# Where the first reads of g and of rounded w_out, and one raw slice of w_out, stand in SP's queue of a retention and SiLU kernel

## The chip, the cores and the metric

The kernel runs on one core of a Trainium2 chip. The metric is the device time of one execution in microseconds, given as the median of several runs. A core has five engines that run side by side, each through its own queue in order: TensorE (PE) multiplies matrices, VectorE (DVE) and ScalarE (ACT) work element by element, GpSimd (POOL) copies here, and SyncE (SP) issues nearly all DMA transfers.

## The reference

Two blocks in a row. A recurrent retention: for each of 4 batches and 8 heads a 64 x 64 state decays and takes in one outer product per step, over 768 steps.

```
for t in range(S):
    state = gamma[None, :, None, None] * state + einsum('bhd,bhe->bhde', k[:, :, t], v[:, :, t])
    y[:, :, t] = scale * einsum('bhd,bhde->bhe', q[:, :, t], state)
x = y.transpose(0, 2, 1, 3).reshape(3072, 512)
h = x @ w_in                       # 512 x 2048
g = h * (1.0 / (1.0 + exp(-h)))    # SiLU
return g @ w_out                   # 2048 x 512
```

q, k and v are float32. The two weight matrices come in as 64-bit floats and are rounded on the chip.

## The kernel before, in words

**Units and groups.** The sequence is cut into 6 chunks of 128 steps. A unit is one chunk of one batch (24 units); its attention is computed in a "visit", whose three phases belong to three units that follow each other. The 4 units of a chunk c give one block xt[c] of 512 rows of x. Group c is what this block costs in the first product: 16 products (c, f), one for each slice f of 128 columns of w_in. The first two groups and half of group 2 are interleaved with the first units; the list `steps` holds the order of the products. From (3,0) on the groups run one after the other, with one visit after every fourth product of groups 3 and 4. Group 5 has no visits.

**Numbers as sums.** A product of float32 quality is made of three products of rounded planes: each operand is split into a high, a low and a mixed plane. `product_in(c, f)` issues eight matmuls into a PSUM bank ha and four into hb (L666). `close_steps` then takes them out: ScalarE copies ha into one of three buffers hs (L676, pool `hpool`), VectorE subtracts hb (L681), ScalarE applies SiLU (L686). The banks ha and hb of successive products go round three banks, so ha of product n+2 takes the bank of hb of product n, and hb of product n+1 the bank of ha of product n.

**g goes through memory.** `put_g(1)` (L689, store at L692) stores all finished tiles of g but the newest and keeps the store's instruction in `stored[0]`. A buffer hs is free again once its store has landed. In the output stage `get(n)` (L698, read at L705) reads the tiles back in order, and `split(n)` (L722) makes three planes of each: ScalarE L731, VectorE L733 and L734. `G_AHEAD` = 4 reads run ahead of the splits, and 3 splits ahead of the products (L1007).

**w_out goes through memory as well.** The 32 slices of both weights (16 of w_in, 16 of w_out) are taken one at a time by `take_w` at the products in the list `takes`. `convert_w` (L226) rounds a slice of 64-bit words in one ScalarE and six VectorE instructions (L202; L205, L208, L212, L215, L218, L223), and asks for the raw slice two further on: at once through `load_w` (L172; a slice of w_out is one transfer of 512 KB, L188), or, when `patient[0]` is set, by putting it into the list `waiting`, which the main loop empties later. A rounded slice of w_out is stored (`store_w`, L288). In group 5 `get_w(f)` (L708, read at L713) reads rounded slices back, `W_READ` = 4 ahead, and `w_out(f)` (L716) splits slice f into planes: ScalarE L120, VectorE L123, ScalarE L126, VectorE L128, and asks for slice f + 4. The low plane goes through one single buffer (tag wl of the pool `conv`).

**Late x.** The block of group 2 is made of values that were stored and are read back by `late_y` (L598) and split by `late_x` (ScalarE L569, VectorE L572 and L575).

**Transposes.** For units from 14 on, q and k are turned by DMA: GpSimd arranges words (`part_t`, L420), SP issues a transposing transfer for q and one for k (`turn_t`, L431), ScalarE joins the words (`join_t`, L438).

**What sets the order.** In the part that the change touches, TensorE's order is the program's. The other engines' queues are put in order by a scheduler when the program is built, which moves an instruction ahead when its inputs and buffers allow it by its own model of time. `with tc.issue_after(ins):` holds it back: what the block issues on the engine of `ins` stays behind `ins`. After the build every engine's queue is fixed.

The main loop (L943 to L985) issues for every product, in this order: the product, `put_g(1)`, `store_w()`, the slice to take, the visit, transposes and loads. In group 5 it adds the reads of w_out at f = 0, a split of w_out for f up to 11, the first four reads of g at f = 10, and the first three splits of g at f = 13 to 15.

Of the kernel before, what the change touches and what calls it, by code (L numbers as in the profile page):

```python
# [33 lines left out]
def kernel(  # L34
# [35 lines left out]
    NF = DF // 128  # L70
# [72 lines left out]
    LATER = 4 * B + 2  # L143
# [115 lines left out]
    taken, patient = [0], [False]  # L259

    def take_w(after=None, parts=False):

        i = taken[0]
        taken[0] += 1
        if i >= 2 * NF:
            return
        with queue(after) if after else ExitStack():
            rounded = convert_w(i)

        def finish():  # L270
            w32 = rounded()
            if i < NF:
                list(split_w(i, w32, "wi", scale, w_sb))
            else:
                to_store.append((i - NF, w32))

        if parts:
            behind_next.append(finish)
        else:
            with queue(after) if after else ExitStack():  # L280
                finish()
# [3 lines left out]
    def store_w():  # L285
        while to_store:
            f, w32 = to_store.pop(0)
            nc.sync.dma_start(out=wo_dram[f], in_=w32)  # L288
# [101 lines left out]
    def scale_k(n):  # L390
        if 0 <= n < len(units):
            t = kqv["k"][n]
            if units[n][0] == NC - 1:
                t = t[:D]
            if 2 * B + 1 < n < 3 * B + 2:

                def half(heads):
                    for h in heads:
                        nc.scalar.activation(out=t[:, h, :], in_=t[:, h, :], func=AF.Copy,
                                             scale=gk[:, units[n][0], h : h + 1])  # L400

                half(range(H // 2))
                behind_copy.append(lambda: half(range(H // 2, H)))
                return
            g = gk[: t.shape[0], units[n][0], :].unsqueeze(2).to_broadcast([t.shape[0], H, D])
            nc.vector.tensor_tensor(out=t, in0=t, in1=g, op=ALU.mult)
# [8 lines left out]
    def part_t(n, after=None):  # L415

        for name, (p, tag, bufs) in (("q", (ld, "kf", 3)), ("k", (one, "kt", 2))):
            src = kqv[name].pop(n) if name == "q" else kqv[name][n]
            t = p.tile([128, 2 * H * D], U16, tag=tag, name=f"{name}p_{n}", bufs=bufs)
            i = nc.gpsimd.tensor_copy(  # L420
                out=t.rearrange("p (w h d) -> p w h d", w=2, h=H),
                in_=src.bitcast(U16).rearrange("p h (d w) -> p w h d", w=2)).ins
            if after is not None:
                tc.add_manual_dep(i, after.name, mybir.DependencyInfo(
                    mybir.DependencyClass.Sync, mybir.DependencyReason.DATA), reason="later")
            planes[name, n] = t

    def turn_t(n):
        for name, (p, tag, bufs) in (("q", (ld, "qf", 2)), ("k", (one, "qt", 3))):
            t = p.tile([128, 2 * HP, C], U16, tag=tag, name=f"{name}w_{n}", bufs=bufs)  # L430
            turned_by[:] = [nc.sync.dma_start_transpose(out=t, in_=planes.pop((name, n))).ins]  # L431
            turned[name, n] = t

    def join_t(name, n):

        to, bufs = (qt, 3) if name == "q" else (kt, 2)
        to[n] = one.tile([128, HP, C], FP32, tag=f"{name}t", name=f"{name}t_{n}", bufs=bufs)
        nc.scalar.copy(out=to[n].bitcast(U16).rearrange("p a (t w) -> p w a t", w=2),  # L438
                       in_=turned.pop((name, n)).rearrange("p (w a) t -> p w a t", w=2))
# [217 lines left out]
    pending, stored = [], []  # L657

    def product_in(c, f):
        close_in(c, f, *multiply(c, f))  # L660
# [28 lines left out]
    def put_g(keep):  # L689
        while len(pending) > keep:  # L690
            c, f, g = pending.pop(0)
            stored[:] = [nc.sync.dma_start(out=g_dram[c, f], in_=g).ins]  # L692
# [5 lines left out]
    def get(n):  # L698
        if n >= len(order):
            return  # L700
        c, f = order[n]
        name = "kvqkvkqv"[n % 8]
        g = ld.tile([128, NT], FP32, tag=f"{name}f", name=f"gr_{c}_{f}",
                    bufs=2 if name == "q" else 3)
        nc.sync.dma_start(out=g, in_=g_dram[c, f])  # L705
        got[n] = g

    def get_w(f):  # L708
        if f < NF:
            tag = "kqkqq"[f % 5]  # L710
            t = one.tile([128, DM], FP32, tag=f"{tag}t", name=f"wr_{f}",
                         bufs=2 if tag == "k" else 3)
            nc.sync.dma_start(out=t, in_=wo_dram[f])  # L713
            w_got[f] = t
# [24 lines left out]
    G_AHEAD = 4  # L739
    W_READ = 4  # L740
# [163 lines left out]
    half = NF // 2  # L904
# [7 lines left out]
    steps = pairs + three + rest + last + groups  # L912
# [22 lines left out]
    turns_at = {first_far + 2: FAR}  # L935
# [7 lines left out]
    for n, (c, f) in enumerate(steps):  # L943
        if n in scales_at:
            behind_next.append(lambda m=scales_at[n]: scale_k(m))
        if n in joins_at:
            behind_copy.insert(0, lambda m=joins_at[n]: [join_t(name, m) for name in "qk"])
        if n in parts:
            behind_next.append(lambda m=parts[n]: part_t(m, taken_out[0]))
        patient[0] = steps.index((3, 0)) <= n < max(turns_at) + 2  # L950
        product_in(c, f)
        put_g(1)
        store_w()
        if (c, f) in takes:
            take_w(taken_out[0], n < len(pairs + three))
        behind.get((c, f), lambda: None)()
        if n in turns_at:
            turn_t(turns_at[n])
            if turns_at[n] >= LATER:
                with tc.issue_after(turned_by[0]):  # L960
                    load("k", turns_at[n] + 1), load("q", turns_at[n] + 1)
        if turns_at.get(n - 1, 0) >= LATER:
            with tc.issue_after(stored[0]):
                load("v", turns_at[n - 1] + 1)
        if turns_at.get(n - 2, 0) >= LATER:
            with tc.issue_after(stored[0]):
                while waiting:
                    load_w(waiting.pop(0))
        for name, m in loads_at.get(n, ()):
            load(name, m)  # L970
        if c == NC - 1:
            if f == 0:
                for i in range(W_READ):
                    get_w(i)
            if f < NF - 4:
                w_out(f)
            if f >= NF - 6:
                if f == NF - 6:
                    for n in range(G_AHEAD):
                        get(n)  # L980
                if f >= NF - S_AHEAD:
                    split(f - NF + S_AHEAD)
    put_g(0)

    for c in range(NC):  # L985
# [9 lines left out]
        for f in range(NF):  # L995
            n = c * NF + f
# [21 lines left out]
        for b in range(B):  # L1018
# [11 lines left out]
            n = 2 if b == B - 1 else 1  # L1030
# [36 lines left out]
```

## Time and profile before

| what | value |
|---|---|
| median of 3 runs | 621.18 us (618.72 to 621.54) |
| profiled execution | 620.76 us, its span 618.9 us |
| TensorE busy | 601.6 us, 97% of the span |
| VectorE, ScalarE, GpSimd busy | 424.6, 315.7, 29.1 us |
| share of TensorE in the chain that ended last | 73% |
| transfers on SP's queue | 102.79 MB in 141392 packets |
| stores of g (96 of 256 KB), median issue to landing | 3.4 us |
| reads of g (96 of 256 KB) | 2.7 us |
| reads of rounded w_out (16 of 256 KB) | 3.5 us |
| raw slices of w_out (16 of 512 KB) | 5.0 us |
| granted TensorE clock | 0.999 |

The span is the time from the first to the last instruction of the profiled execution; 1.9 us of its own time lie around it. Busy times are sums over the whole span and hide that stages differ. The chain that ended last is followed back from the last instruction, at each step to what released it; a DMA in it is a transfer that something waited for. In the tables by stretches the columns are each engine's busy time in the stretch with the number of its instructions, and then the granted clock, the DMA share and the rate. Products of group 5 begin at 309.24 us and 2.72 us apart; the output products begin at 352.85 us.

### The profile page before, as it was taken

How to read it: one execution, taken by the hardware profiler on the slowest of the kernel's cores; microseconds unless marked ns; L12 is line 12 of the kernel's file. 1: busy time of each engine (PE TensorE's matmuls, PEld its weight loads, DVE VectorE, ACT ScalarE, POOL GpSimd, SP SyncE). 2: the span in 40 equal slices, each digit the busy share in tenths (PEclk: the TensorE clock that was granted, in tenths of full speed). 3: DMA queues.
4: the chain of work that ended last, by engine and by line, in shares of the span. 5: the costliest groups of instructions: out<-in, count | busy, mean ns of one | idle time of the engine just before them, and what ended most of it. 6: DMA issues, size and time to landing. Idle time of an engine off the chain costs nothing.

```text
span 618.9 us, 13462 instructions
## 1 busy us (share of the span) xinstructions
PE 601.6 (97%) x5360; PEld 494.6 (80%) x5360; DVE 424.6 (69%) x731; ACT 315.7 (51%) x595; POOL 29.1 (5%) x85
## 2 busy tenths in 40 slices
PE   6898999999999999999999999999999999999997
PEld 5777787888778888887788888888888888888886
DVE  4998889889977777785699783645635453654631
ACT  6677896676667567665588642312221221412311
POOL 3000000100031111120000000000000000000000
PEclk9999999999999999999999999999999999999999
DMA  9998874784789699999777552533524433442301
GB/s 193 221 227 208 220 216 158 202 241 169 250 217 222 184 265 241 275 233 292 273 227 257 193 147 68 169 104 92 180 70 132 140 102 103 141 132 89 116 1 68
DMA packets 144334, 108.88 MB, mean 176 GB/s; under 512 B 101136, under 2 KB 109584, under 8 KB 144272
## 3 DMA queue, kind: packets, MB, share of 16 engines
q1 hardware_dynamic: 141392, 102.79, 59.7%
q10 hardware_dynamic: 2880, 5.24, 2.3%
q8 instruction: 42, 0.69, 0.5%
q14 instruction: 20, 0.16, 0.1%
HBM read 66.06 MB, written 36.70 MB: 166 GB/s over the span
## 4 chain that ended last, share of the span: by engine, by line
PE 73%; DVE 5%; DMA 2%; ACT 2%; issue 1%; SPq 1%; DVEq 0%; POOLq 0%; ACTq 0%
PE o L1007 21%; PE ha L666 18%; PE oa L1007 14%; PE hb L666 10%; PE ob L1007 7%; PE y L513 2%; DMA gd<-g 1%; DVE g L681 1%; DMA yr<-yd 1%; SPq L431 1%; PE sc L474 1%; PE sc L464 1%; DVE ca L218 1%; DVE xt L572 0%; ACT g L676 0%
## 5 line engine op out<-in xcount | busy, mean ns | idle before, releaser
L666 PE MATMUL ha<-xt,wi 128*128 128x512 f32 x768 | 193.7, 394 | 1.3 <-ACT xt L569 0.7
L666 PEld LDWEIGHTS ha<-xt,wi 128*128 128x128 f32 x768 | 141.8, 188 | 33.5 <-ACT xt L569 1.1
L1007 PE MATMUL o<-wo,gs 128*128 128x512 f32 x564 | 143.2, 389 | 0.0
L733 DVE TENSOR_TENSOR gs<-gr,gs 128x512 fp32r<-128x512 f32 x96 | 62.1, 685 | 90.3 <-ACT gs L731 90.3
L1007 PEld LDWEIGHTS o<-wo,gs 128*128 128x128 f32 x564 | 105.9, 188 | 21.9
L731 ACT ACTIVATE gs<-gr 128x512 fp32r<-128x512 f32 x96 | 53.6, 621 | 134.2 <-issue 131.9
L1007 PE MATMUL oa<-wo,gs 128*128 128x512 f32 x376 | 115.8, 389 | 0.0
L666 PE MATMUL hb<-xt,wi 128*128 128x512 f32 x384 | 103.2, 390 | 1.9 <-ACT g L676 0.9
L681 DVE TENSOR_TENSOR g<-g,hb 128x512 f32<-128x512 f32 x96 | 65.6, 683 | 37.1 <-ACT g L676 24.7
L666 PEld LDWEIGHTS hb<-xt,wi 128*128 128x128 f32 x384 | 71.8, 188 | 18.4 <-ACT g L676 1.8
L686 ACT ACTIVATE g<-g 128x512 f32<-128x512 f32 x96 | 60.1, 627 | 46.2 <-DVE g L681 46.2
L1007 PEld LDWEIGHTS oa<-wo,gs 128*128 128x128 f32 x376 | 70.6, 188 | 14.7
L1007 PE MATMUL ob<-wo,gs 128*128 128x512 f32 x188 | 73.7, 392 | 0.0
L676 ACT ACTIVATE g<-ha 128x512 f32<-128x512 f32 x96 | 56.7, 591 | 28.5 <-PE ha L666 11.9
L734 DVE SCALAR_TENSOR_TENSOR gs<-gs 128x512 fp32r<-128x512 f32 x96 | 62.0, 683 | 0.0
L1007 PEld LDWEIGHTS ob<-wo,gs 128*128 128x128 f32 x188 | 35.3, 188 | 8.7 <-DVE o L1025 1.6
L202 ACT ACTIVATE ca<-wf 128x512 f32<-128x512 f32 x32 | 21.4, 668 | 8.0 <-DVE cw L223 5.0
L218 DVE SCALAR_TENSOR_TENSOR ca<-wf,ca 128x512 f32<-128x512 uint32 x32 | 22.7, 710 | 0.5
L1024 ACT ACTIVATE o<-o 128x512 f32<-128x512 f32 x10 | 6.0, 598 | 33.4 <-PE o L1007 33.0
L482 DVE TENSOR_TENSOR am<-sc,decay 128x512 f32<-128x512 f32 x24 | 16.5, 688 | 9.1 <-PE sc L474 9.0
L212 DVE SCALAR_TENSOR_TENSOR cs<-ca,cs 128x512 uint32<-128x512 uint32 x32 | 22.1, 691 | 0.9
L513 PE MATMUL y<-qt,mid 64*64 64x64 f32 x384 | 20.2, 224 | 1.8 <-POOL token L385 1.8
(93 smaller groups left out, 568.4 us busy)
## 6 DMA issues: line engine op xcount, KB each, us to landing
gd<-g SPq DMA_DIRECT2D x96, 256.0 KB, 3.4
gr<-gd SPq DMA_DIRECT2D x96, 256.0 KB, 2.7
wf<-in_moe_w_out_dram SPq DMA_DIRECT2D x16, 512.0 KB, 5.0
out_dram<-o ACTq DMA_DIRECT2D x20, 256.0 KB, 2.1
wf<-in_moe_w_in_dram SPq DMA_DIRECT2D x16, 256.0 KB, 4.2
wf<-in_moe_w_in_dram SPq DMA_DIRECT2D x32, 128.0 KB, 4.0
kf<-in_k_dram SPq DMA_DIRECT2D x16, 256.0 KB, 4.3
qf<-in_q_dram SPq DMA_DIRECT2D x16, 256.0 KB, 4.1
```

The costliest lines, as they stand in the source:

```text
L202: nc.scalar.activation(out=a.bitcast(FP32), in_=hi.bitcast(FP32), func=AF.Abs, scale=65536.0)
L212: nc.vector.scalar_tensor_tensor(out=s, in0=a, scalar=3, in1=s, op0=ALU.logical_shift_left, op1=ALU.bitwise_or)
L218: nc.vector.scalar_tensor_tensor(out=p.bitcast(FP32), in0=lo, scalar=2.0 ** -52, in1=p.bitcast(FP32), op0=ALU.mult, op1=ALU.mult)
L513: i = nc.tensor.matmul(yp[ts(e, D), o, a, :], lhsT=lhsT, rhs=rhs, start=(e, o) not in started, stop=True, skip_group_check=True).ins
L666: nc.tensor.matmul(hb if i == 2 else ha, lhsT=w_sb[f][:, i, ts(kk, 128)], rhs=xt[c][:, i, kk, :], start=kk == 0 and i != 1, stop=kk == KIN ...
L676: copied[:] = [nc.scalar.activation(out=hs, in_=ha, func=AF.Copy, scale=ONE_E).ins]
L681: taken_out[:] = [nc.vector.tensor_tensor(out=hs, in0=hs, in1=hb, op=ALU.subtract).ins]
L686: nc.scalar.activation(out=hs, in_=hs, func=AF.Silu)
L731: nc.scalar.activation(out=t[:, 0, :], in_=g, func=AF.Copy, scale=HALF)
L733: nc.vector.tensor_tensor(out=t[:, 1, :], in0=g, in1=high, op=ALU.subtract)
L734: nc.vector.scalar_tensor_tensor(out=t[:, 2, :], in0=t[:, 1, :].bitcast(FP32), scalar=-1.0 / EPS, in1=high, op0=ALU.mult, op1=ALU.add)
L1007: nc.tensor.matmul(o, lhsT=g, rhs=wo[f][:, i, :], start=f == 0 and i != 1, stop=f == NF - 1 and i != 0)
```

## The change

Three edits in the main loop.

- Ahead of product (0,15) `patient[0]` is now set as well, so the raw slice that the conversion taken there asks for (slice 19, a slice of w_out) goes into `waiting` instead of being loaded at once. The list is emptied at product (2,8) too, behind the newest store of g.
- The first four reads of rounded w_out, at (5,0), are held behind the newest store of g.
- The first four reads of g, at (5,10), are held behind the newest store of g.

```diff
-        patient[0] = steps.index((3, 0)) <= n < max(turns_at) + 2
+        patient[0] = (c, f) == (0, NF - 1) or steps.index((3, 0)) <= n < max(turns_at) + 2
         product_in(c, f)
         put_g(1)
         store_w()
...
-        if turns_at.get(n - 2, 0) >= LATER:
+        if turns_at.get(n - 2, 0) >= LATER or (c, f) == (2, half):
             with tc.issue_after(stored[0]):
                 while waiting:
                     load_w(waiting.pop(0))
...
             if f == 0:
-                for i in range(W_READ):
-                    get_w(i)
+                with tc.issue_after(stored[0]):
+                    for i in range(W_READ):
+                        get_w(i)
             if f < NF - 4:
                 w_out(f)
             if f >= NF - 6:
                 if f == NF - 6:
-                    for n in range(G_AHEAD):
-                        get(n)
+                    with tc.issue_after(stored[0]):
+                        for n in range(G_AHEAD):
+                            get(n)
```

In the built program the first four reads of g move from ahead of the store of product (4,6) to behind the store of (5,9). The first reads of w_out move from between the stores of (4,7) to (4,13) to behind the store of (4,15), where the first five stand in one row. The raw slice moves from ahead of the last store of w_out and the last read of y, near 166 us, to between the two transposes for unit 15. With the reads, the splits that use them move in the queues of ScalarE and VectorE.

## The prediction

> **What bounds the kernel now.** I read the busy table and the chain first, then the pieces of the chain at the two places that the diff touches, then the table by stretches, then VectorE's timeline.
>
> ```profile
> PE 601.6 (97%) x5360; PEld 494.6 (80%) x5360; DVE 424.6 (69%) x731; ACT 315.7 (51%) x595; POOL 29.1 (5%) x85
> PE 73%; DVE 5%; DMA 2%; ACT 2%; issue 1%; SPq 1%; DVEq 0%; POOLq 0%; ACTq 0%
> ```
>
> TensorE is busy for 97% of the span and carries 73% of the chain. A product of this kernel is 12 matmuls that start 0.227 us apart, 2.72 us in all (the timeline shows ha's eight in 1.81 us and hb's four in 0.91), and almost all of them follow each other without a break. An edit that only moves transfers can win only what TensorE loses to late data, and can cost only new waits. So I look for the breaks. The pieces of the chain in group 4:
>
> ```profile
> 283.25 0.53 SPq L705
> ...
> 285.30 6.70 DMA gd<-g
> ...
> 292.11 0.60 ACT g L676
> ...
> 292.76 1.20 PE hb L666 x4
> ```
>
> Four reads of g (L705) are issued from 283.25 to 285.20, and the store of product (4,6) behind them takes 6.70 us to land. Product (4,9) needs that store's buffer (hs has three), ScalarE's copy waits until 292.11, and TensorE, which wants the bank that the copy empties, has no hb before 292.76. From the start of product (4,10)'s ha at 289.78 to its hb are 2.98 us, where the same place in the other visits takes 1.95: 1.03 us lost, and 0.12 us of slower restart (hb's four take 1.03, not 0.91). And in group 2:
>
> ```profile
> 168.22 4.71 DMA yr<-yd
> ...
> 172.95 0.64 ACT xt L569
> ...
> 173.61 1.13 DVE xt L572
> ...
> 174.76 1.42 DVE xt L575
> ...
> 176.23 1.21 PE hb L666 x4
> ```
>
> The last read of y stands behind a raw slice of w_out (issued 166.43, landed 171.66) and needs 4.71 us; the first such read took 2.70. Product (2,8) waits for its last plane: ha to hb 2.42 us instead of 1.95, and 0.14 for the restart.
>
> Now the stage that receives the moved work, group 5 (309.24 to 352.85):
>
> ```profile
> core 0: us, PE busy (x) PEld busy (x) DVE busy (x) ACT busy (x) POOL busy (x), PEclk, DMA share, GB/s
> ...
> 309.00:325.00 16.00, 16.00 (x72) 13.25 (x71) 15.95 (x29) 13.89 (x27) 0.00 (x0) 1.00 0.71 231
> 325.00:341.00 16.00, 16.00 (x72) 13.16 (x71) 16.00 (x30) 13.53 (x25) 0.00 (x0) 1.00 0.77 258
> 341.00:353.00 12.00, 12.00 (x54) 9.83 (x53) 8.26 (x14) 7.61 (x13) 0.00 (x0) 1.00 0.64 217
> ```
>
> VectorE is busy for 31.95 of the first 32 us, and has 3.7 us to spare only in the last 12. TensorE never waits here, but only because VectorE starts at once and never pauses. This is the row that decides.
>
> [...] the copy of (4,9) held up the copies behind it for 4.26 us. [...] The landings of SP's transfers in this trace come in the order of issue, in backlog some 0.65 us apart for 256 KB (292.00, 292.63, 293.26, 293.91). [...] lone stores of g land after 2.0 us here. [...]
>
> **The change, part by part.** No instruction is added or removed; orders on SP, ScalarE and VectorE change, TensorE's and GpSimd's do not. Times are in the clock of the kernel before.
>
> *The raw slice (SP).* It leaves its place ahead of the last store of w_out and the last read of y, and is issued between the two transposes of unit 15, ahead of one read of q, a transpose and a store of g. The read of y then lands at about 168.22 + 2.7 to 3.1 = 171.1 us instead of 172.93; ScalarE's plane follows its copy of 171.04, VectorE's two planes end before hb is due at 173.81 + 1.95 = 175.76. Gain 0.47 + 0.14 = **0.6 us** (0 to 1.0: the break of 0.46 us before 168.84 is VectorE's and stays). Cost of the new place: 512 KB lengthen the queue by 1.25 us (293.91 to 295.16) to 2.64 us (169.02 to 171.66). What counts is the second transpose for unit 15's k: it landed at 192.26 and ScalarE took it at 193.75, so 1.5 us are free. The DMA share from 177 to 204 is over 1, so the delay may survive; it costs 0 to 1.1 us. I take **0.2**.
>
> *First four reads of g (SP, then ScalarE, VectorE).* They go from group 4 to behind the store of (5,9). The store of (4,6) is then issued at 283.25, right behind the transposes, and lands about 0.65 us after the transpose of 285.23: at 285.9. ScalarE is free for the copy of (4,9) at 287.8, TensorE needs it at 291.7. The break goes: **-1.15 us**. Nothing is late next: the following store waits for its SiLU of 284.25. Their splits (4 x 0.61 us on ScalarE, 8 x 0.60 on VectorE, at its spacing) move from the start of group 5 to its end, where the output products need the first at 352.85; read at about 337, split before (5,13): hidden.
>
> *First reads of rounded w_out.* Five reads (the fifth is the one that the first split asks for) now stand in one row behind the store of (4,15), one raw slice and one store of w_out, and ahead of the store of (5,0). In the trace before, the six transfers behind that raw slice (issued 312.23, landed 315.89) landed at 316.75, 318.14, 318.79, 319.44, 320.10 and 321.28. The slice waits for L218, which no longer stands behind a split of g (0.6 us). In those places now land: w_out's store 316.2, reads 0 to 4 at 317.5, 318.2, 318.8, 319.5, 320.7, the store of (5,0) later still. Before, read 0 had been there since 293; ScalarE and VectorE began on it at 312.5.
>
> So VectorE has only the subtractions of (5,0), (5,1), (5,2) from 312.2 on, and ends the third at 318.3. In its queue between that and the subtraction of (5,3) then stand three splits of w_out (6 x 0.60 us) and one whole conversion (0.34 + 0.34 + 0.60 + 0.34 + 0.60 + 0.60 = 2.82): 6.42 us. Before, two of the splits were done ahead of (5,2)'s. One pause comes on top: the single low buffer (conv has one) is freed by ScalarE only after its plane of read 2 (318.8), about 320.4, 0.2 us after VectorE is there. (5,3)'s subtraction ends at 318.3 + 6.42 + 0.2 + 0.68 = 325.6. TensorE needs its bank for (5,5) at 322.84. That is 2.8 us, with the restart **+2.95 us**. From there to (5,12)'s subtraction VectorE has nine subtractions (5.4 us), nine splits (10.8) and two conversions (5.6), 21.8 us to 347.4, and TensorE reaches the end of (5,12) at 344.85 + 2.95 = 347.8: no second break. Bounds: 2.6 without any wait for reads, 6.8 in the rival below.
>
> SP's own waits: read 5 waits for VectorE to release buffer 0 (318.9), and the stores of (5,1) and (5,2) wait behind it; they land at about 323 and 324, for copies that the break has put off anyway. At most 0.5 us, inside the 2.95.
>
> Sum: -0.6 + 0.2 - 1.15 + 2.95 = **+1.4 us**. Against the profiled execution (span 618.9, its time 620.76) that is 620.3 and 622.2. The median of the three runs, 621.18, lies 0.42 above that execution; on it the forecast is 622.6 us.
>
> **The rivals.** A measurement of this kernel tells about 0.5%, 3.1 us, from no change (its three runs lie 2.8 us apart).
>
> *A, forecast: the break of group 5 outweighs those of groups 2 and 4.* 622.6; within 0.5%. Chance 0.50.
>
> *B, slower: reads come late.* Same place, but the reads of w_out land as the four reads of g did at 286.07, 287.20, 289.20 and 291.35, up to 2.15 us apart. Read 2 lands at about 323.7, ScalarE frees the low buffer at 324.4, (5,3)'s subtraction ends at about 329: a break of 6.8, in all +5.3, 626.4 us. For it: raw slice, store and five reads make 2 MB in front of one store. Against it: no transposes or k, q, v loads share group 5's queue, and reads of w_out landed 0.63 to 1.2 us apart elsewhere. It decides from the point where the break is over 4.65 us, read 2 later than about 321. Chance 0.34.
>
> *C, the break is smaller.* If VectorE gets at the splits earlier than I think, the wins remain: down to -1.75 us, 619.4. Against it: the queue is fixed at build time and the 6.42 us are in it. Chance 0.13, of which hardly anything passes 3.1 us: all breaks of TensorE after 160 us make some 3 us.
>
> *D, nothing happens,* since the ordering edges could leave the built order as it was. The built program shows the reads at their new places, so 0.03, at 621.2.
>
> **How the numbers follow.** Faster by over 0.5% 0.03 (from C, with the spread of the runs); slower by over 0.5% 0.36 (B, and 0.02 of A with a full loss of 1.1 us at the transposes); the rest, 0.61, within. The range goes from C (619.6) to B's far end (626.4).
>
> **What would show it.** Right: no wait of ScalarE's L676 for a store of g near 291; the last read of y landing in about 3 us, and hb of (2,8) on time; VectorE idle between 312 and 318; a break of about 3 us before ha of (5,5), ended by L681. Wrong: TensorE unbroken in group 5 (C), the break over 4.7 us there (B), or a break near 190 to 200 behind the transposes.

## The result and the profile after

The changed kernel takes 628.12 us, the median of 6 runs (624.47 to 629.76), against 621.36 us of the kernel before in the same session (6 runs, 618.72 to 623.34). The ratio is 1.0107, its 95% interval 1.0079 to 1.0135: slower by 1.1%, where +1.4 us was forecast. The profiled execution took 628.61 us, 7.85 us over the one of before; its span is 626.7 us.

First the changed kernel's page, its busy table and the shares of the chain that ended last:

```profile
PE 606.0 (97%) x5360; PEld 496.7 (79%) x5360; DVE 425.4 (68%) x731; ACT 316.7 (51%) x595; POOL 30.0 (5%) x85
PE 66%; DMA 6%; DVE 6%; ACT 3%; issue 2%; SPq 1%; DVEq 0%; ACTq 0%; POOLq 0%
```

TensorE's share of the chain falls from 73% to 66%, that of DMA rises from 2% to 6%: TensorE waits more for transfers. But TensorE is also *busy* 4.4 us longer (601.6 before) with the same 5360 matmuls. So waits cannot be all of it; some matmuls took longer.

The chain says where. These are its pieces in groups 3 and 5 (start, duration, what):

```profile
200.98 2.66 DMA gd<-g
...
203.70 1.36 ACT kt L438
...
206.09 1.20 PE hb L666 x4
...
222.45 6.89 DMA wf<-in_moe_w_out_dram
...
231.63 1.21 PE hb L666 x4
...
321.53 3.69 DMA gd<-g
...
327.01 0.69 DVE g L681
...
327.74 3.59 PE ha L666 x8
331.33 0.92 PE hb L666 x4
332.25 1.81 PE ha L666 x8
...
350.25 5.90 DMA gd<-g
...
356.26 0.61 ACT g L676
...
356.91 1.21 PE hb L666 x4
```

Read from below: a store of g that took 5.90 us holds up ScalarE's copy and TensorE's hb at 356.91. At 327.74 ha's eight matmuls take 3.59 us, where the same eight take 1.81 us one product later. Ahead of them VectorE's subtraction (L681) came late. The two breaks in group 3 go back to late transfers as well.

Since TensorE's order is the same in both kernels, the start of each product's ha can be subtracted, one profile from the other. The delay of the changed kernel grows in these places only: 0.78 us in the first 110 us, 1.57 at hb of (3,0) and (3,1), 0.97 at hb of (3,7), -1.15 at hb of (4,10), 2.71 ahead of ha of (5,5), 1.63 in ha of (5,5), 1.36 at hb of (5,14). The sum is 7.87 us, the whole difference of the two spans.

The place that was predicted shows best in VectorE's timeline (start, duration, instruction, and in brackets the idle time before it):

```profile
314.56 0.68 DVE L681 TENSOR_TENSOR g<-g,hb 128x512 f32<-128x512 f32 x1
317.12 0.69 DVE L681 TENSOR_TENSOR g<-g,hb 128x512 f32<-128x512 f32 x1 [1.88 <-ACT g L676]
319.84 0.69 DVE L681 TENSOR_TENSOR g<-g,hb 128x512 f32<-128x512 f32 x1 [2.03 <-PE hb L666]
320.45 0.69 DVE L123 SCALAR_TENSOR_TENSOR wol<-wr,wo 128x512 f32<-128x512 f32 x1
...
327.01 0.68 DVE L681 TENSOR_TENSOR g<-g,hb 128x512 f32<-128x512 f32 x1
```

VectorE is idle for 1.88 and 2.03 us between the subtractions of (5,0), (5,1) and (5,2), because the splits that filled this time before have no data yet: read 0 of w_out lands at 319.39. Then it works from 320.45 to 327.01 without a pause, 6.56 us, before it comes to the subtraction of (5,3). The table by stretches (columns as in the one of before) gives the rest:

```profile
309.00:325.00 16.00, 15.94 (x71) 12.89 (x70) 11.95 (x22) 10.08 (x17) 0.00 (x0) 1.00 0.69 222
325.00:341.00 16.00, 13.80 (x55) 10.99 (x54) 14.08 (x25) 12.10 (x22) 0.00 (x0) 0.89 0.71 230
341.00:353.00 12.00, 12.00 (x55) 9.87 (x54) 11.00 (x20) 9.07 (x18) 0.00 (x0) 1.00 0.75 226
...
325.00:327.70 2.70, 0.55 (x3) 0.10 (x1) 2.70 (x6) 2.21 (x4) 0.00 (x0) 0.97 0.84 265
327.70:331.40 3.70, 3.66 (x9) 2.93 (x10) 3.17 (x5) 1.85 (x4) 0.00 (x0) 0.56 0.92 311
```

In the first 16 us of group 5 VectorE did 11.95 us of work instead of 15.95. Then TensorE stood still for 2.2 us, and in the 3.7 us after that its granted clock was 0.56: half clock for 3.413 us. A second such period, from 27.19 to 30.61 us, lies in the first 110 us, and the profile of before shows none ahead of its last output product. At half clock 3.413 us do the work of 1.7, so the two explain about 3.4 of the 4.4 us that TensorE is busy longer (an estimate).

### The profile page after: what moved, and what is told of

The parts are those of the page before. It is cut to its first block, busy times and chain, and to the rows that moved or that the text cites. A ratio compares the mean times of both kernels' runs of the same rounds, so it can differ in the third digit from the quotient of the medians.

```text
span 626.7 us, 13463 instructions
## 1 busy us (share of the span) xinstructions
PE 606.0 (97%) x5360; PEld 496.7 (79%) x5360; DVE 425.4 (68%) x731; ACT 316.7 (51%) x595; POOL 30.0 (5%) x85
## 4 chain that ended last, share of the span: by engine, by line
PE 66%; DMA 6%; DVE 6%; ACT 3%; issue 2%; SPq 1%; DVEq 0%; ACTq 0%; POOLq 0%
PE o L1009 20%; PE ha L666 15%; PE oa L1009 14%; PE hb L666 8%; PE ob L1009 7%; DMA gd<-g 2%; DVE g L681 1%; DMA kw<-kp 1%; DMA wf<-in_moe_w_out_dram 1%; PE y L513 1%; DMA qw<-qp 1%; DMA yr<-yd 1%; ACT g L676 1%; ACT g L686 1%; DVE ca L218 1%
## 5 line engine op out<-in xcount | busy, mean ns | idle before, releaser
L666 PE MATMUL ha<-xt,wi 128*128 128x512 f32 x768 | 196.5, 398 | 3.2 <-DVE g L681 2.5
L666 PEld LDWEIGHTS ha<-xt,wi 128*128 128x128 f32 x768 | 143.7, 190 | 36.2 <-DVE g L681 3.4
L681 DVE TENSOR_TENSOR g<-g,hb 128x512 f32<-128x512 f32 x96 | 65.6, 684 | 43.5 <-ACT g L676 27.7
L575 DVE SCALAR_TENSOR_TENSOR xt<-xt 128x512 fp32r<-128x512 f32 x28 | 20.9, 745 | 0.7
```

The costliest lines, as they stand in the source:

```text
L575: nc.vector.scalar_tensor_tensor(out=x[2], in0=x[1].bitcast(FP32), scalar=-1.0 / EPS, in1=x[0].bitcast(FP32), op0=ALU.mult, op1=ALU.add)
L666: nc.tensor.matmul(hb if i == 2 else ha, lhsT=w_sb[f][:, i, ts(kk, 128)], rhs=xt[c][:, i, kk, :], start=kk == 0 and i != 1, stop=kk == KIN ...
L681: taken_out[:] = [nc.vector.tensor_tensor(out=hs, in0=hs, in1=hb, op=ALU.subtract).ins]
```

## The experiments

The twelve experiments belong to three sessions. Those of one session share their runs of the kernel before, whose median was 620.98 us (E1 to E4, 44 runs), 619.59 (E5 to E8, 7 runs) and 622.66 (E9 to E12, 51 runs); since these differ by 3 us, a time is compared inside its session. The table gives, for each profile, how far it fell behind the first profile of before at each place (us; gains are negative). An empty cell is under 0.1.

| kernel | first 110 us | hb (2,8) | hb (3,0), (3,1) | hb (3,7) | hb (4,3) | hb (4,10) | ahead of ha (5,5) | in ha (5,5) | hb (5,14) |
|---|---|---|---|---|---|---|---|---|---|
| changed | 0.78 | | 1.57 | 0.97 | | -1.15 | 2.71 | 1.63 | 1.36 |
| E8 changed again | 1.26 | | 0.51 | | 0.36 | -1.15 | 2.81 | 1.45 | 1.74 |
| E12 before again | 1.44 | -0.18 | | | | -1.13 | | | |
| E1 slice alone | -0.29 | -0.62 | 1.05 | 0.65 | 0.46 | -1.14 | | | |
| E2 reads of w_out alone | -0.19 | | | | | -1.14 | 3.77 | 1.73 | |
| E3 reads of g alone | 4.02 | | | | | -1.12 | | | 1.50 |
| E4 both sorts of reads | -1.31 | -0.13 | | | | -1.16 | 2.71 | 0.14 | 1.50 |
| E6 changed, pause filled | | | | 0.42 | 1.70 | -1.14 | 2.97 | 0.13 | 0.18 |
| E7 changed, conversions later | 1.62 | | 1.84 | | 0.44 | -1.14 | 0.43 | | 1.54 |
| E9 slice behind y | 2.90 | | | | 0.16 | | | | |
| E10 g one by one | 4.50 | -0.17 | | | 1.12 | -1.15 | | | |
| E11 both mended | 1.66 | -0.62 | | | | -1.14 | | | |

(E7 loses 2.63 us more between (5,6) and (5,14), E6 2.1 us in the output stage. E5 is left out: up to the output stage it is the kernel before. The gains of 0.13 to 0.18 us at hb of (2,8) only undo an equal delay at ha of (2,8).) The first column differs by 5.8 us between kernels that are equal there; it is chance and comes back under the last heading.

### E1: the raw slice alone

```diff
-        patient[0] = steps.index((3, 0)) <= n < max(turns_at) + 2
+        patient[0] = (c, f) == (0, NF - 1) or steps.index((3, 0)) <= n < max(turns_at) + 2
...
-        if turns_at.get(n - 2, 0) >= LATER:
+        if turns_at.get(n - 2, 0) >= LATER or (c, f) == (2, half):
```

> Only the raw slice of w_out is moved. Theory (the profile after, read place by place): the slice costs where it goes and brings nothing where it leaves. The two products behind unit 15's second transpose lose 1.0 to 1.6 us together, because ScalarE's join for k waits for the reads and transposes queued behind the slice; hb of (2,8) still comes 2.4 us after its ha, as before. Time: kernel before plus 1 to 1.6 us; with the break at (4,10) still there and no break at (5,5). Rival 1: the late transposes of the profile after were its own variation; then the slice alone is within 0.5 us of before, and (2,15) to (3,1) run unbroken. Rival 2: the 0.97 us lost at (3,7), where the reads of stored w_in or w_out words came late, belongs to the slice too; then that break is here as well, and the time is plus 2 to 2.6 us.

Measured: 622.42 us, 1.44 over before; ratio 1.0029 (1.0008 to 1.0049). The delays of group 3 are here: those at (3,0) and (3,1) are in four of the five profiles with this move (changed, E1, E7, E8, not E6), the one at (3,7) in three (changed, E1, E6), and neither is in any of the nine other profiles. They go with the slice, though they do not come every time. The break at (4,10), expected to stay, is missing (see E12). What the expectation got wrong is also who waits. TensorE's timeline, at hb of (3,1):

```profile
204.93 1.98 PE L666 MATMUL ha<-xt,wi 128*128 128x512 f32 x8
207.67 1.19 PE L666 MATMUL hb<-xt,wi 128*128 128x512 f32 x4 [0.76 <-ACT g L676]
```

and ScalarE's:

```profile
204.27 0.63 ACT L686 ACTIVATE g<-g 128x512 f32<-128x512 f32 x1 [0.75 <-DVE g L681]
207.02 0.60 ACT L676 ACTIVATE g<-ha 128x512 f32<-128x512 f32 x1 [2.12 <-PE ha L666]
```

ScalarE is idle for 2.12 us ahead of the copy of (3,0), and this is not the join. The view names TensorE's ha as what ended the wait, but that ha ended long before; the copy needs the buffer of (2,13), whose store was issued at 201.02 and landed at 206.92. In the kernel before the same store went out at 199.80 and landed at 204.87, 0.83 us before the copy. So behind the 512 KB put in at 177 between the transposes this store, 24 us further on, went out 1.22 us later and took 0.83 us longer (one pair of profiles).

The gain at (2,8) is here too, as predicted at first, but in neither profile of the changed kernel; of the seven profiles with the slice moved, E1 and E11 alone have it. In the changed kernel's two profiles the last read of y itself did get quicker: 3.83 and 3.72 us, where it took 4.71 and 5.05 in the two profiles of before. What was late was the read ahead of it, which stands before the slice's old place as well: 4.82 and 4.71 us, against 3.06 in the first profile of before and 3.21 here. It takes 4.3 to 4.9 us in twelve of the fourteen profiles; why, is left open. Its planes then filled VectorE when the last ones were due (from 172.25 to 174.38 us in the changed kernel).

### E2: the reads of rounded w_out alone

```diff
-                for i in range(W_READ):
-                    get_w(i)
+                with tc.issue_after(stored[0]):
+                    for i in range(W_READ):
+                        get_w(i)
```

> Only the first reads of rounded w_out are moved. Theory: this part alone makes the wait ahead of ha of (5,5), 2.2 us of idle TensorE or 2.7 us of delay, and the idle time is followed by about 3.4 us at half clock, 1.6 us more. Time: kernel before plus 4.3 us; the break at (4,10) remains and none appears near (5,15). The reads of g stay early here, so that their splits stand ahead in VectorE's queue; if they take VectorE's time between 312 and 318 us, the wait for (5,5) may be up to 1 us longer or shorter. Rival 1: the slow eight matmuls of (5,5) in the profile after were a throttle of that execution and not a consequence of the wait; then the wait is here and ha of (5,5) takes 1.95 us: plus 2.7 us. Rival 2: the wait for (5,5) needs the moved reads of g as well; then this kernel is within 0.5 us of before.

Measured: 626.32 us, 5.34 over before; ratio 1.0103 (1.0071 to 1.0135). This part makes most of the loss. TensorE's timeline:

```profile
321.99 1.19 PE L666 MATMUL hb<-xt,wi 128*128 128x512 f32 x4 [1.18 <-ACT g L676]
325.32 3.23 PE L666 MATMUL ha<-xt,wi 128*128 128x512 f32 x8 [2.14 <-DVE g L681]
```

Ahead of the known pause stands another of 1.18 us, at hb of (5,4), where the changed kernel loses 0.2 (together 3.77 us, where 2.7 with a margin of 1 us was expected), and ha's eight matmuls take 3.23 us, half clock again. The reads of g are still early here, so their splits fill VectorE's queue in this stretch. The break at (4,10), which was expected to stay, is not there (see E12). Rival 2 falls; rival 1 doesn't show here, and E4 and E5 come back to it.

### E3: the first reads of g alone

```diff
-                    for n in range(G_AHEAD):
-                        get(n)
+                    with tc.issue_after(stored[0]):
+                        for n in range(G_AHEAD):
+                            get(n)
```

> Only the first four reads of g are moved. Theory: the break at (4,10) goes (-1.15 us), and the four reads stand directly ahead of the store of product (5,10), which lands about 6 us after its issue, so that the copy of (5,13) and hb of (5,14) or (5,15) wait: +1.1 to 1.4 us. Time: within 0.5 us of before. Rival 1 (the prediction's view, nothing is late next): no break near (5,15), time before minus 1.15 us. Rival 2: the break near (5,15) needs the delay of 4.3 us at (5,5) to come about; then this kernel too is 1.15 us faster than before.

Measured: 622.52 us, 1.54 over before; ratio 1.0027 (1.0010 to 1.0045). The chain of waits:

```profile
346.83 5.83 DMA gd<-g
...
352.77 0.61 ACT g L676
...
353.42 1.19 PE hb L666 x4
```

The store behind the four reads lands 5.83 us after its issue, without any delay at (5,5): rivals 1 and 2 fall. The break has the same cause as the one shown of group 4, a store behind four reads; it was moved, not removed. At its new place it comes nearly every time (five of six profiles).

### E4: both sorts of reads, the slice as before

The diffs of E2 and E3 together.

> Both sorts of first reads moved, the raw slice left where it was: the changed kernel without its first part. Theory: changed kernel minus the slice's 1.0 to 1.6 us: before -1.15 (break of group 4) +2.7 (wait) +1.6 (half clock) +1.3 (store behind four reads) = before plus 4.5 us, some 626 us. Rival 1: the slice also causes the 0.97 us at (3,7) and the 0.8 us at the start; then before plus 4.5 as well, but the changed kernel stands 3 us and more above this one. Rival 2: the parts are not independent (the moved reads of g leave VectorE free ahead of (5,5)); then the wait at (5,5) is shorter here than with the reads of w_out alone, by more than 0.5 us.

Measured: 626.35 us, 5.37 over before; ratio 1.0086 (1.0056 to 1.0117). With E1's 1.44 this gives 6.81 us; the whole change measured 6.76. (So close an agreement is luck, as E1's interval alone is 2.5 us wide.) Rival 2 came true: the wait is 2.71 us, and 3.77 in E2, where splits of g stand in VectorE's queue. In its profile the pause is the same and the half clock is missing, as TensorE's timeline says:

```profile
323.06 2.12 PE L666 MATMUL ha<-xt,wi 128*128 128x512 f32 x8 [2.20 <-DVE g L681]
```

Pauses of 2.1 to 2.2 us, with half clock behind them in three profiles (changed, E8, E2) and without in this one. In each profile the periods of half clock begin and end on one grid of 3.413 us ("window" is used here for the stretch between two of its lines). In the changed kernel's profile they begin at 27.19 and 327.56 us, 88 times 3.413 us apart. Where the lines fall differs from one execution to the next: at 324.15 and 327.56 us there, at 322.05 us here. Laid over the table by stretches, this pause is cut in two by the line at 322.05:

```profile
318.60:322.00 3.40, 2.21 (x9) 1.18 (x7) 3.40 (x7) 2.27 (x5) 0.00 (x0) 1.00 0.81 254
322.00:325.40 3.40, 2.34 (x10) 1.95 (x11) 3.31 (x6) 2.95 (x6) 0.00 (x0) 1.00 0.96 250
```

TensorE is busy for 65% and 69% of the two windows. In the changed kernel nearly the whole pause fell into one window, busy for 39%:

```profile
324.15:327.56 3.41, 1.33 (x5) 0.67 (x4) 3.41 (x7) 2.22 (x5) 0.00 (x0) 1.00 0.87 242
```

### E5: pauses of four lengths in the output stage

```diff
+    def pause(done, then, k):
+        sync = mybir.DependencyInfo(mybir.DependencyClass.Sync, mybir.DependencyReason.DATA)
+        for j in range(k):
+            i = nc.gpsimd.memset(pad, 0.0).ins
+            if j == 0:
+                tc.add_manual_dep(i, done.name, sync, reason="pause")
+        tc.add_manual_dep(then, i.name, sync, reason="pause")
...
+                    if (b, i) == (0, 0) and n % 4 == 2:
+                        pause(last_mm[0], mm, (4, 7, 10, 13)[n // 4 % 4])
```

> The kernel before, with 24 pauses of TensorE added in the output stage: at every fourth step TensorE waits for a chain of 4, 7, 10 or 13 writes of GpSimd to a spare tile (about 1, 1.6, 2.2 and 2.8 us, from 0.20 us a write). The result is untouched. In the profiles so far the periods of half clock all begin on a fixed grid of 3.413 us, and a pause of 2.2 us was followed by one in the changed kernel and in the kernel with the reads of w_out alone (busy share of the 3.413 us window ahead: 0.39 and 0.37) and by none in the kernel with both sorts of reads (the pause lay across two windows with 0.64 and 0.70). Theory: the clock is halved for one window exactly after a window in which TensorE was busy for less than about half, so that pauses of 1.0 us never do it, of 1.6 us now and then, of 2.2 us in some half of the cases and of 2.8 us nearly always; each costs 1.7 us. Rival: the length of the pause alone decides, with a fixed bound near 2.2 us; then all six of 2.8 us do it and those of equal length behave alike, wherever they lie on the grid. Time: 620.8 plus 6 times (1.0 + 1.6 + 2.2 + 2.8) = 46 us, plus 1.7 for each period of half clock, 8 to 12 of them: 680 to 688 us.

Measured: 713.82 us in one run. The pauses came out longer than planned and there were 23 (the last place is not reached by this loop): 1.17, 1.95, 2.74 and 3.52 us. None of the six of 1.17 us was followed by half clock, five of the six of 1.95, five of the six of 2.74, and all five of 3.52. Two pauses of 1.95 us, in the table by stretches, each followed by the next window:

```profile
369.00:372.40 3.40, 1.68 (x7) 1.40 (x8) 0.00 (x0) 0.00 (x0) 1.32 (x7) 1.00 0.32 101
372.40:375.80 3.40, 3.40 (x16) 2.79 (x16) 0.00 (x0) 0.00 (x0) 0.00 (x0) 1.00 0.00 0
427.00:430.50 3.50, 1.55 (x7) 1.05 (x6) 0.51 (x1) 0.00 (x0) 1.43 (x7) 0.99 0.37 140
430.50:433.90 3.40, 3.40 (x9) 2.67 (x8) 0.00 (x0) 0.00 (x0) 0.00 (x0) 0.50 0.00 0
```

The first pause left TensorE busy for 0.50 of its exact window (1.68 of the 3.40 us shown), the second, equally long, for 0.43. Over all profiles, after the first 110 us: a window at full clock with a share of 0.48 or less was followed by half clock (15 of 15 here; 0.39 in the changed kernel, 0.48 in E8 and 0.37 in E2 at (5,5); the one exception is the last window of E10 with matmuls, 0.44), and none with 0.50 or more was. A pause of 2.74 us across a line (0.67 and 0.53) had no effect. So the length alone does not decide; the share of the window fits all cases but the one. The "about half" of the expectation was the author's estimate, put between the shares seen until then (0.39 and 0.37 with half clock behind them, 0.64 and 0.70 without). The 15 are not 15 independent cases: the pauses come back to the same places of the grid, with shares near 0.32, 0.40 and 0.43. The time missed the expectation because the pauses were longer, and because the half clock lasted for two windows behind four of the pauses of 2.74 us and all of 3.52: the first of the two was still partly idle (0.63 to 0.81).

### E6: the pause filled

```diff
+        if (c, f) == (5, 5):
+            spare = banks("q", "spare", 1)[:, 0]
+            for i in range(9):
+                nc.tensor.matmul(spare, lhsT=w_sb[5][:, 0, ts(0, 128)], rhs=xt[5][:, 0, 0, :],
+                                 start=True, stop=True)
         product_in(c, f)
```

> The changed kernel with nine matmuls added ahead of product (5,5), into a bank that nobody reads: they need nothing that is late, so they run in the pause of 2.2 us there. The result is untouched. Theory: the wait for VectorE's subtraction stays and ha of (5,5) starts as late as before, but TensorE is busy in the window ahead, so ha's eight matmuls take 1.85 to 2.0 us and not 3.6. Rival: the half clock came from something else than the pause; then it is seen here too.

Measured: 627.13 us in one run. TensorE's timeline:

```profile
324.43 2.21 PE L954 MATMUL spare<-xt,wi 128*128 128x512 f32 x9
326.79 2.11 PE L666 MATMUL ha<-xt,wi 128*128 128x512 f32 x8
```

ha starts as late as before (2.97 us) and then runs at full clock; it costs 0.13 us instead of 1.63. The windows of the grid, placed by this profile's one change of clock, at 625.37 us:

```profile
321.58:324.99 3.41, 3.08 (x14) 2.24 (x13) 3.41 (x7) 2.74 (x6) 0.00 (x0) 1.00 0.84 265
324.99:328.41 3.42, 3.27 (x15) 2.39 (x14) 3.42 (x6) 2.77 (x6) 0.00 (x0) 1.00 0.87 286
```

Without the nine matmuls the second window would have been busy for 0.47 (worked out from the trace by leaving them out), just inside the shares that were followed by half clock. Since half clock can stay out behind an open pause as well (E4), this one profile proves little alone; it fits E5, which carries the proof. The time isn't comparable: TensorE in E6 also waits twice in the output stage, at 403.53 and 579.35 us, where 2.1 us are lost that no kernel without an added bank or pause loses; that the added bank did it, by shifting the round of the banks, is a guess that was not shown. The break at (5,14) is nearly gone in this execution, one of 1.58 us of idle time appears at (4,3): both come and go.

### E7: the conversions later

```diff
-    takes += [(5, f) for f in (2, 5, 8)]
+    takes += [(5, f) for f in (4, 6, 8)]
```

> The changed kernel, with the two conversions of raw slices that stood at products (5,2) and (5,5) moved to (5,4) and (5,6). The reads of w_out stay where they are and land as late. In VectorE's queue there are then five instructions of splits, 3.0 us, and no conversion between the subtractions of (5,2) and (5,3), instead of 6.4 us. Theory (the queue behind the late reads, not the reads themselves, makes the wait): the subtraction of (5,3) ends near 322.3 in the clock of the kernel before, TensorE wants it at 322.84, and the pause of 2.2 us ahead of (5,5) is gone; what VectorE lost while it waited shows as 0.1 to 0.6 us at (5,6) to (5,9). Time: the changed kernel minus 2.2 to 4.3 us, so 624 to 626 us. Rival: the landing of the reads decides; then TensorE waits at (5,5) as long as in the changed kernel (2 us and more). Second rival: the lost time of VectorE only comes back later as one pause of 2 us or more between (5,6) and (5,12).

Measured: 628.15 us against 619.59; ratio 1.0137 (1.0107 to 1.0167). No gain: the expectation missed. The wait at (5,5) did shrink from 2.7 to 0.43 us with the reads just as late. But the table by stretches shows what then happened:

```profile
309.00:325.00 16.00, 15.93 (x71) 12.86 (x69) 10.55 (x18) 10.38 (x18) 0.00 (x0) 1.00 0.63 214
325.00:341.00 16.00, 15.40 (x64) 11.63 (x64) 16.00 (x30) 12.93 (x25) 0.00 (x0) 1.00 0.74 235
```

VectorE is busy for all of the second stretch, and TensorE loses 0.3 to 0.7 us at each of the products (5,7) to (5,12), with a rest 2.63 us by (5,14). With 0.43 and 0.05 that is 3.1 us: the second rival, only spread out. The first rival falls. Since there is no half clock either, group 5 loses 1.2 us less up to there than in the changed kernel (3.1 against 2.71 and 1.63); the time doesn't show this, and its interval of 3.7 us is too wide to. The order in VectorE's queue mostly decided where its lost time was paid. That the lost time is the 3.9 us in which VectorE had nothing to do fits here, but is not shown as a rule: between ha of (5,0) and ha of (5,5) VectorE is idle for 4.05 us in the changed kernel and for 1.15 in E2, which waits longer. The whole queue counts, its work and its idle time.

### E8 and E12: the changed kernel and the kernel before once more

No edit.

> The changed kernel once more, for a second profile. What belongs to the change must come again: the break of 2.2 us ahead of (5,5), one of about 1 us behind the store of (5,10), the delay of 1.0 to 1.6 us behind unit 15's transposes, no break at (4,10). What is chance may differ: the half clock after (5,5), which depends on where the pause falls in the grid of 3.413 us, the 0.78 us lost in the first 60 us, the missing gain at (2,8), and perhaps the 0.97 us at (3,7).

> The kernel before once more, for a second profile. If the break at (4,10) belongs to it, TensorE loses 0.9 to 1.2 us there again, because the store of (4,6) behind four reads of g lands 6 us and more after its issue; if it was chance (it was missing in the kernel with the slice alone and in the one with the reads of w_out alone, which both leave those reads where they were), it is not seen here, and the term of -1.15 us was never the change's to win. At (2,8) hb should come 2.4 us after ha again.

Measured: 627.80 and 621.07 us in one run each. The changed kernel shows the same breaks at (5,5), in its half clock and at (5,14) again; the one at (3,7) is absent, that of the transposes is 0.51 us where 1.0 to 1.6 was expected, and one at (4,3) is new. What makes those at (3,7) and (4,3) come and go is left open. The kernel before does *not* show its break at (4,10) a second time; its chain there:

```profile
291.29 2.04 PE ha L666 x8
293.33 0.91 PE hb L666 x4
```

Over the six profiles that keep four reads of g ahead of the store of (4,6) (before twice, E1, E2, E5, E9) two have the break; of the eight with the reads moved none has. The store tells why. Behind four reads it takes 4.73 to 6.70 us, and ScalarE's copy of (4,9) starts 0.1 us after its landing in all six; TensorE feels it only in the two where it took longest, 6.70 (before) and 6.19 (E9). With the reads moved it takes 2.4 to 2.5 us, and lands at least 2.3 us ahead of the copy. So the edit does remove the break, but on average that is worth about a third of 1.15, 0.4 us (an estimate from these counts).

### E9: the slice behind the last read of y

```diff
-        if turns_at.get(n - 2, 0) >= LATER:
-            with tc.issue_after(stored[0]):
+        if turns_at.get(n - 2, 0) >= LATER or (c, f) == (1, NF - 4):
+            with tc.issue_after((y_read if c == 1 else stored)[0]):
```

(`y_read` keeps the last read of y, and `patient[0]` is set as in E1.)

> Only the raw slice is moved, and only past two transfers: behind a store of w_out and the last read of y, instead of behind the first store of g after the two transposes of unit 14's successor. Nothing else in any queue differs from the kernel before. Theory: the last read of y no longer stands behind 512 KB, so hb of (2,8) may be on time, as it was with the slice alone (gain 0.6 us there, none in the two profiles of the changed kernel); and since the slice isn't among the transposes of units 15 and 16, the delays at (2,15) to (3,1), (3,7) and (4,4) that all five profiles with the moved slice show in some mixture (0.9 to 2.5 us together) do not come. Time: before minus 0 to 0.7 us. Rival: any move of the slice makes the later transfers late; then it costs 1 us and more, as the slice alone did (1.44).

Measured: 621.42 us against 622.66; ratio 0.9987 (0.9969 to 1.0005). The delays of group 3 are gone: the place between the transposes costs, not the move as such. The gain at (2,8) failed again, for the reason given under E1 (the read ahead took 4.72 us). And it has the break at (4,10): the store of (4,6) takes 6.19 us.

### E10 and E11: the reads of g one by one, and both parts mended

```diff
+            if NF - 8 <= f < NF - 8 + G_AHEAD:
+                with tc.issue_after(stored[0]):
+                    get(f - NF + 8)
             if f >= NF - 6:
-                if f == NF - 6:
-                    for n in range(G_AHEAD):
-                        get(n)
                 if f >= NF - S_AHEAD:
-                    split(f - NF + S_AHEAD)
+                    with tc.issue_after(stored[0]):
+                        split(f - NF + S_AHEAD)
```

(The splits of the output stage are held behind `stored[0]` in the same way. E11 adds the edit of E9.)

> The reads of g moved to the end of group 5 as in the change, but one for each product from (5,8) on, each behind the newest store, and the later ones too; the reads of w_out and the raw slice stay as before. Theory: no store then stands behind four reads, so that the break of 1.4 to 1.7 us at (5,15), seen in five of six profiles with the moved reads, is gone, and so is the one at (4,10). Time: before minus 1.15 us if the break at (4,10) belongs to the kernel before, the same as before if it was chance in its one profile (it was missing in the two kernels that leave those four reads where they were). Rival: the stores of group 5's end land late whatever stands ahead of them, one read or four; then a break of over 1 us near (5,15) stays, and the time is that of the kernel with only the reads of g moved (1.5 us over before).

> The raw slice behind the last read of y, and the reads of g one by one at the end of group 5; the reads of w_out as before. Theory: the two parts add up, and leave TensorE without a break over 0.3 us from 110 us to the output stage: before minus 0 to 1.8 us. Rival: they don't add up, since later loads meet the transposes; then not faster than the better one of the two alone.

Measured: E10 621.58 us, ratio 0.9986 (0.9969 to 1.0002); E11 621.44, ratio 0.9986 (0.9966 to 1.0006), both against 622.66. With one read ahead of a store instead of four there is no break at (5,14), nor at (4,10): the store of (5,10) takes 3.17 and 3.35 us, where behind four reads it took 5.41 to 5.97. E11's profile has no idle time of TensorE over 0.31 us between 110 us and the output stage. E11 also has the gain of 0.6 us at (2,8). Both stand 1.1 to 1.2 us under before, which the interval doesn't separate from nothing. Against the changed kernel the difference is clear, as the intervals of the two ratios lie apart (E11 up to 1.0006, the change from 1.0079). E10 has a break of 1.1 us at (4,3) without the slice's move, so that break isn't the slice's alone.

## Why the prediction was wrong

For the largest term the mechanism, the sign and the size were right: forecast 2.8 us, measured 2.71 and 2.81; (5,3)'s subtraction ending at 325.6, measured 325.5 (327.70 less the 2.19 us that the changed kernel was behind there); 6.42 us of queue, measured 6.56. Read 2 landed at 321.18, 319.0 in the clock of before, so rival B didn't happen; that the time came near B's 626.4 us is coincidence. The sum failed in four of its terms. Together they make 5.8 us of the 6.5 by which the profile missed the forecast of 1.4; the rest is chance in the first 110 us (0.78), less 0.1 at the wait itself.

- **"With the restart +2.95"**: the restart was taken at 0.14 us, from breaks of about 1 us. Behind this pause it was 1.63 us, because TensorE's clock was halved for 3.413 us. It isn't certain: it came in three of the four profiles with the pause of 2.2 us left open. What it went with is shown by E4 and E5, the busy share of the window ahead: 0.39 in the changed kernel and 0.48 or less in E5 with half clock, 0.65 and 0.69 in E4 without. E6 fits.
- **"Nothing is late next" and "hidden"** for the four reads of g: the step followed the splits, which were indeed hidden, and not the store behind the reads. The store of (5,10) stood behind four reads as the store of (4,6) had, and cost 1.36 us (1.36 to 1.74 in five of six profiles with the reads in a row). E10 and E11 remove it by spreading the reads. The profile of before had shown the price: 6.70 us for a store behind four reads.
- **The slice's new place at 0.2 us (0 to 1.1)**: the step looked at one instruction, the second transpose with 1.5 us to spare. Transfers were still late 24 us after the slice, and in E1 the store of (2,13), which had 0.83 us to spare before, was the one that its copy waited for. Cost 1.57 and 0.97 us in the profile, the largest single error; 1.44 in E1's time.
- **The slice's gain of 0.6 us**: none in the changed kernel, and in two of seven profiles with the slice moved. The last read of y became quicker (3.83 us instead of 4.71), though not the 2.7 to 3.1 expected; and the read ahead of it, quick in the one profile that was read, is slow in most.

The term of -1.15 us came out to a hundredth in the comparison of the two profiles, and was still half a mistake: the break is in the profile of before by chance (2 of 6). All four errors point the same way, so the time lay above the range, whose upper end was that of one rival with the other terms unchanged. Two slips of the sum matter little: B's break of 6.8 us doesn't follow from its own end of about 329 (329 less 322.84 is 6.2, or about 6.3 with the restart), so its far end should have been about 0.5 us lower; and C is put at 619.4 us in one place and 619.6 in the other. Nor does the profile's sum hold for every run: E1 and E4 add up to 6.81 us in their medians, against 6.76 of the change, while single profiles differ by more than 1 us in the terms that chance decides.

## What to carry to other kernels

If a stage's second engine is as busy as its first, price a late transfer by adding up that engine's queue from the landing to the instruction that someone waits for; here this met the wait within 0.1 us. Reordering the queue mostly spread the wait (E7: 2.71 us became 0.43, and 2.63 more came later). When reads are moved, look at the next store behind them in the same queue and at who waits for its buffer; here a row of four cost 1.36 to 1.74 us where it stood, and one by one no break was left there (E10, E11). And before a break in a single profile is booked as a gain, look whether a second profile has it.

## What the runs showed of the hardware

- **Half clock on a grid of 3.413 us.** All periods of half clock (granted clock 0.50) ahead of a kernel's last matmul last 3.413 or 6.827 us, on one grid in each profile. After the first 110 us, pauses of 1.95 to 2.2 us were followed by half clock when they left one window busy for 0.48 or less (0.39 in the changed kernel, 0.37 in E2, 0.48 in E8), and not when they left 0.50 (E5) or 0.65 and 0.69 (E4); one of 2.74 us across a line (0.67 and 0.53, E5) was not either. The pauses lay among matmuls of 512 columns.
- **Part of the scatter of this kernel's time goes with half clock.** Each period takes 1.7 us and lowers the mean granted clock of a 620 us execution by 0.0027 (both estimates: half of 3.413 us, and that over 620). From 20 to 60 us, where TensorE waits often and its matmuls are of several sizes, windows with a share of 0.27 to 0.55 occur; those under 0.5 were all followed by half clock, of those at 0.5 to 0.55 some (in the changed kernel the one of 0.53 at 23.78 us). Of the 44 runs of before in the first session the 19 with a mean clock of 0.999 or more have a median of 619.65 us, the 7 at 0.992 or less 623.21; over all 44 the clock accounts for about half of the variance of the time, over the 51 of the third session for less (0.38).
- **A delay in SP's queue, 24 us on.** In E1, 512 KB stood between two transposes, and a store 24 us further on was issued 1.2 us later and took 0.8 us longer than before, in a stretch where the share of the DMA engines is over 1 (1.13 from 177 to 190 us in E1, 1.02 before). It is one pair of profiles, and E6, with the slice in the same place, lost nothing at (3,0) and (3,1).
- **A store behind reads.** A store of 256 KB took 4.7 to 6.7 us behind four reads of 256 KB in one queue (4.73 to 6.70 that of (4,6), 5.41 to 5.97 that of (5,10)), 3.2 to 3.4 with one read ahead (that of (5,10) in E10 and E11), and about 2.0 alone (2.00 in the kernel before, issued at 308.15).
